# Spreading a layer's last weight conversions evenly, and moving pair preparation and reciprocal transposes by one step

## The chip, the cores and the metric

One core of a Trainium2 chip runs the whole program: clustered attention, a dense two-matrix layer, and a layer of eight experts. The metric is the device time of one execution in microseconds (us). TensorE is PE in the rows (PEld: its weight loads), VectorE DVE, ScalarE ACT, GpSimd POOL, SyncE SP; SPq is the SyncE queue, which issues most DMAs. "Granted clock" is the share of TensorE's full clock that the chip allowed: 1.00 is 2.4 GHz, 0.5 is 1.2 GHz.

## The reference, cut to what matters

```python
# attention: batch 2, 8 heads, 768 positions, head_dim 64, 16 clusters
q_assign = argmax(q_n @ c_n.T); k_assign = argmax(k_n @ c_n.T)   # normalised
scores = where(q_assign == k_assign, q @ k.T / sqrt(64), -1e9)
attn = exp(scores - max); attn = attn / (sum(attn) + 1e-9)
x = attn @ v                             # to 1536 tokens x 512
# first layer: 512 -> 2048 -> 512
h = x @ w_in; x = maximum(0.01 * h, h) @ w_out
# second layer: one of 8 experts (512 -> 1024 -> 512) per token, where x @ w_skip > 0
y = x + gate * (relu(x @ w1[e]) @ w2[e])
```

The weights of the first layer, `w_in` and `w_out`, are 64-bit floats in memory. The program takes them as pairs of 32-bit words and makes 32-bit floats of them; this is the "conversion".

## The kernel before, in words

**Attention.** Two heads form a pair, and there are eight pairs. A pair has 12 steps, r = 0 to 11, 96 in all: two halves of 384 queries, in each half three blocks of 128 queries by two heads. A step s gives each engine a fixed list, in the order of the loop `for s in range(NSTEP + 12 + LAG)`, and every engine works its list strictly in order:

- TensorE: scores of step s (`sps`, L366); six transposes of the exponentials of step s - 3 into two PSUM tiles `tps` (L423); every sixth step the transpose of the reciprocal sums, `rcps` (L401), into a tile of the same two; in even steps the value product (`avps`, L438); then one item of the preparation.
- VectorE: the row maximum `st` of the scores (L369), one or two operations of a conversion, the reciprocals, and operations of the preparation.
- ScalarE: `Abs` of a conversion in every fourth step (L557), a copy of the preparation, the two copies of `tps` to SBUF (L430), the copy of `rcps`, the exp (L384), and in steps 2 and 8 the copy `xr` of the finished value product (L446).
- GpSimd: splits into high and low parts of the next pair, the load `rb` of the reciprocals (L409) from memory, where SyncE stored them, and their product with `xr` (L453).

The preparation of a pair lies in the steps of the two pairs before it. It is a table of (step, slot, function): four raw transposes (`rawps`, L179) with a copy each in the step behind, the cluster scores (`asps`, L231), their transposes (`scps`, L243), the choice of the cluster in four VectorE operations (`argmax_0` to `argmax_3`), the transposes of the one-hot mask (`ohps`, L290), its scaling (`mk`, L296) and its DMAs. `plan(d)` writes this table with all steps relative to d. The slot "pb" stands at the end of a step on TensorE, "a0" near its start, "d" on VectorE behind the maximum.

**First layer.** 48 iterations i, 16 for each of three blocks of 512 tokens. An iteration has `up` of i (12 matmuls, L658), `down` of i - 2 (12 matmuls, L765), then `m1_act`: `lk` on ScalarE (L749), `g` on VectorE (L750), `gh` on ScalarE (L751), `gl` on VectorE (L752); then the splits of the weights of i + 2: `whii` and `whio` on ScalarE (L632, L643), `wloi` and `wloo` on GpSimd (L634, L644). `up` of i needs `whii` and `wloi` of i.

Of 32 pieces of the weights (128 rows each) 20 are converted during attention. The last 12 are converted in the first iterations by `conv_next(n)`, which brings the count of converted pieces up to n, two at a time: two `Abs` on ScalarE, then four VectorE operations for each piece (L559, L561, L564, L570). After each two it issues the next loads. The load of the fourth of the 12 goes into a tile (`stg`, two buffers) that the first of the 12 occupies. Pieces 5 to 8 of the 12 are read by `split_i` at the end of iteration 10, pieces 9 to 12 by `split_o` from there on.

Of the kernel before, what the change touches and what calls it, by code (L numbers as in the profile page):

```python
# [25 lines left out]
def kernel(  # L26
# [284 lines left out]
    def plan(d):  # L311
        return [
            (d - 8, "pb", raw_pe, 0), (d - 7, "a0", raw_act, 0), (d - 7, "pb", raw_pe, 1),
            (d - 6, "a0", raw_act, 1), (d - 6, "pb", raw_pe, 2), (d - 5, "a0", raw_act, 2), (d - 5, "pb", raw_pe, 3),
            (d - 4, "a0", raw_act, 3), (d - 4, "pb", assign_pe, None),
            (d - 3, "a0", assign_act, None), (d - 3, "pb", argmax_pe, None),
            (d - 2, "d", argmax_0, None), (d - 2, "d", argmax_1, None), (d - 1, "d", argmax_2, None),
            (d, "d", argmax_3, None), (d + 1, "pb", mask_pe, None), (d + 2, "d", mask_dve, None),
            (0, "a0", raw_split, 0), (1, "a0", raw_split, 1), (2, "a0", raw_split, 2), (3, "a0", raw_split, 3),
            (3, "d", exchange, 0), (5, "d", exchange, 1), (max(d + 2, 5), "d", mask_dma, None),  # L320
        ]

    PREP = plan(0)
    PREP0 = [(3, "a0", assign_act, None), (3, "pb", argmax_pe, None), (4, "d", argmax_0, None), (4, "d", argmax_1, None),
             (5, "d", argmax_2, None), (6, "d", argmax_3, None)]
    PREP1 = [(1, "pb", assign_pe, None), (2, "a0", assign_act, None), (2, "pb", argmax_pe, None), (3, "pb", argmax_0, None), (4, "pb", argmax_1, None), (5, "d", argmax_2, None), (6, "pb", argmax_3, None), (7, "pb", mask_pe, None), (8, "d", mask_dve, None),
             (8, "d", mask_dma, None)]
    PREPS = {0: PREP0, 1: PREP1, 2: plan(4), 3: plan(2)}

    def prep(p, r, slot):  # L330
        if p >= NP:
            return
        for rr, sl, f, arg in PREPS.get(p, PREP):
            if rr == r and sl == slot:
# [262 lines left out]
    def preps(p, r, slot):  # L597
        prep(p + 1, r, slot)
        if r >= 4:
            prep(p + 2, r - 12, slot)  # L600
# [65 lines left out]
    def load_next(n):  # L666
        while nxt[0] < min(n, len(pieces)):
            load_piece(*pieces[nxt[0]])
            nxt[0] += 1

    def conv_next(n):
        while nxt[1] < min(n, len(pieces)):
            two = pieces[nxt[1]:nxt[1] + 2]
            for i_ in range(5):
                for pc in two:
                    convert_op(*pc, i_)
            nxt[1] += 2
            load_next(nxt[1] + (2 if wsp[0] is None else 4))

    for s in range(NSTEP + 12 + LAG):  # L680
        p, r = divmod(s, 12)
        if s < NSTEP:
            st_scores(s)
        conv_step(s, 0)
        preps(p, r, "a0")
        preps(p, r, "pa")
        if 0 <= s - LAG < NSTEP:
            st_transpose(s - LAG)
            st_evac(s - LAG)
        gf, rf = divmod(s, 6)  # L690
        if 0 < gf <= NSTEP // 6:
            if rf == 2:
                recip_rows(gf - 1)
            elif rf == 3:
                nc.sync.dma_start(rscr[gf - 1], rrow_t.pop(gf - 1))
        g, kt = divmod(s - 6 - LAG, 6)
        if 0 <= g < NSTEP // 6 and kt % 2:
            st_av(g, kt - 1)
            st_av(g, kt)
        if s < NSTEP:  # L700
            st_exp(s)
        if 0 <= g < NSTEP // 6 and kt == NT - 1:
            av_evac(g)
            av_split(g)
        if 0 <= g < NSTEP // 6 and kt == 3:
            recip_load(g)
        if 0 < gf <= NSTEP // 6 and rf < 2:
            recip(gf - 1, rf)
        preps(p, r, "d")
        preps(p, r, "pb")  # L710
        if r == 10 and p + 1 < NP:
            load_v(p + 1)
        conv_step(s, 1)
        if s == NSTEP:
            att_a.release()
            rt = pool("rt", "left")
            ring_b[0] = pool("ring_b", "left")
            wip[0] = pool("wi", "left")
            for c in range(NDIR // 4, NPC // 4):
                load_f32(c)  # L720
            load_next(2)
        if s == NSTEP + 4:
            for i in range(3):
                split_i(i)
# [301 lines left out]
    for i in range(NI):  # L1026
        if i == 14:
            r_consts()
        if i >= 2:
            m1_up(i)  # L1030
        for f, arg in sorted(r_tasks.get(i, ()), key=lambda x: x[1]):
            f(arg)
        step_gen(i, 0)
        if i >= 2:
            m1_down(i - 2)
        m1_act(i)
        step_gen(i, 1)
        if i + 2 < NI:
            if i:
                split_i(i + 2)  # L1040
            split_o(i + 2)
            g_, j_ = divmod(i + 2 - 2 * NFC, 4)
            if g_ >= 0 and j_ == 3:
                load_chunk(8 + 2 * g_)
                load_chunk(9 + 2 * g_)
        conv_next(i + 3 if i % 2 else 0)

    lb = NBLK - 1
    LT = lb * TPB
# [370 lines left out]
```

## Time and profile before

| What | Value |
| --- | --- |
| median of 3 runs | 690.68 us (690.42 to 690.96) |
| the profiled execution, its own time | 689.63 us |
| its span, first to last instruction | 687.9 us |
| TensorE busy | 636.7 us, 93% of the span |
| ScalarE busy | 423.8 us, 62% |
| VectorE busy | 407.4 us, 59% |
| GpSimd busy | 278.2 us, 40% |
| mean granted clock | 0.985 |

The shares are means over stages with different limits, so they only say where to look: TensorE is the engine whose idle time can be worth something, and there are 51 us of it. What ended each of its idle stretches stands in the list of waits and in the rows in order of time, where a bracket such as "[0.39 <-ACT pt L430]" gives the idle time of the engine ahead of an instruction and what ended it.

### The profile page before, as it was taken

Reading aid. Unit: us, or ns where it says so; the run is one execution under the profiler, and the core shown is the slowest. Engines: PE = TensorE matmul, PEld = TensorE weight load, DVE = VectorE, ACT = ScalarE, POOL = GpSimd, SP = SyncE. Lnnn points to the kernel's source line nnn. Section 1 sums busy time; section 2 is a strip of 40 time slices with the busy share of each in tenths; the row PEclk is TensorE's granted clock in tenths of the full one; section 3 lists DMA queues with packets and bytes.
Section 4 is the critical chain, followed back from the end, with each engine's and each line's share of the span. In section 5 each row is a group of like instructions: output and inputs, shape, how many; then the busy total and the mean of one; then the engine's idle time right before and its main releaser. Section 6 shows DMA issues by size and latency. Waiting matters only on the chain. (4 is left out here: it accounts for less than half of the span.)

```text
span 687.9 us, 10140 instructions
## 1 busy us (share of the span) xinstructions
PE 636.7 (93%) x3587; PEld 491.8 (71%) x3587; DVE 407.4 (59%) x687; ACT 423.8 (62%) x824; POOL 278.2 (40%) x295
## 2 busy tenths in 40 slices
PE   5898999999999999499999999999999979989994
PEld 3676766666766666378888888788787868767873
DVE  5755858686776653767523213623226348999991
ACT  5887888897888885254445444445444436757870
POOL 4233636264553324363554444444444273002321
PEclk9999999999999999889999999999999999999997
DMA  8763764767656354221003000006303349989950
GB/s 196 184 189 95 196 163 140 187 172 193 167 153 171 111 183 144 104 111 61 1 3 122 1 1 0 1 0 245 122 3 122 123 163 362 339 280 333 357 192 25
DMA packets 62659, 98.31 MB, mean 143 GB/s; under 512 B 27593, under 2 KB 31659, under 8 KB 62224
## 3 DMA queue, kind: packets, MB, share of 16 engines
q1 hardware_dynamic: 59040, 88.13, 41.5%
q0 software_dynamic: 3568, 9.52, 4.2%
q8 instruction: 29, 0.48, 0.3%
q14 instruction: 22, 0.18, 0.1%
HBM read 72.47 MB, written 11.65 MB: 122 GB/s over the span
## 5 line engine op out<-in xcount | busy, mean ns | idle before, releaser
L369 DVE TENSOR_REDUCE st<-sps 128x1 f32<-128x768 f32 x96 | 91.5, 954 | 66.7 <-PE sps L366 66.3
L430 ACT ACTIVATE pt<-tps 128x384 f32<-128x384 f32 x192 | 84.8, 503 | 19.2 <-PE tps L423 18.6
L384 ACT ACTIVATE pr<-sps,st 128x768 f32<-128x768 f32 x96 | 87.7, 914 | 13.9 <-DVE st L369 13.4
L750 DVE TENSOR_TENSOR g<-ups,lk 128x512 f32<-128x512 f32 x48 | 33.1, 689 | 105.9 <-ACT lk L749 105.8
L634 POOL TENSOR_TENSOR wloi<-rawb,whii 128x512 fp32r<-128x512 f32 x36 | 46.7, 1298 | 115.4 <-ACT whii L632 115.4
L658 PE MATMUL ups<-xh,whii 128*128 128x512 f32 x192 | 76.0, 396 | 7.9 <-ACT whii L632 7.9
L423 PE MATMUL tps<-ident,pr 128*128 128x128 f32 x576 | 78.7, 273 | 0.5 <-ACT pt L430 0.5
L658 PE MATMUL ups<-xh,wloi 128*128 128x512 f32 x192 | 75.7, 394 | 1.4 <-POOL wloi L634 1.3
L658 PE MATMUL ups<-xl,whii 128*128 128x512 f32 x192 | 75.6, 394 | 0.0
L765 PE MATMUL acc<-whio,gh 128*128 128x512 f32 x184 | 73.4, 399 | 0.0
L765 PE MATMUL acc<-wloo,gh 128*128 128x512 f32 x184 | 71.8, 390 | 0.1
L423 PEld LDWEIGHTS tps<-ident,pr 128*128 128x128 f32 x576 | 68.4, 140 | 5.1 <-ACT pt L430 1.6
L438 PE MATMUL avps<-pt,vnat 128*64 128x384 f32 x384 | 71.9, 498 | 0.0
L765 PE MATMUL acc<-whio,gl 128*128 128x512 f32 x184 | 71.8, 390 | 0.0
L751 ACT ACTIVATE gh<-g 128x512 fp32r<-128x512 f32 x48 | 30.4, 632 | 51.9 <-DVE g L750 51.9
L749 ACT ACTIVATE lk<-ups 128x512 f32<-128x512 f32 x48 | 28.5, 593 | 50.9 <-PE ups L658 50.9
L752 DVE TENSOR_TENSOR gl<-g,gh 128x512 fp32r<-128x512 f32 x48 | 34.6, 721 | 33.5 <-ACT gh L751 33.5
L453 POOL TENSOR_TENSOR xr<-xr,rb 128x384 f32<-128x384 f32 x16 | 16.0, 1002 | 81.2 <-ACT xr L446 77.9
L658 PEld LDWEIGHTS ups<-xh,whii 128*128 128x128 f32 x192 | 36.6, 190 | 16.3 <-ACT whii L632 8.3
L644 POOL TENSOR_TENSOR wloo<-rawb,whio 128x512 fp32r<-128x512 f32 x36 | 47.0, 1304 | 0.8 <-ACT whio L643 0.8
L1171 POOL DMA_INDIRECT out_dram<-y,idx_s x8 | 13.6, 1695 | 76.8 <-DVE y L1169 36.0
L658 PEld LDWEIGHTS ups<-xh,wloi 128*128 128x128 f32 x192 | 36.6, 190 | 10.2 <-POOL wloi L634 2.6
(294 smaller groups left out, 1388.8 us busy)
## 6 DMA issues: line engine op xcount, KB each, us to landing
rawb<-in_moe_w_dram SPq DMA_DIRECT2D x26, 1024.0 KB, 6.9
stg<-in_moe_w_in_dram SPq DMA_DIRECT2D x16, 512.0 KB
stg<-in_moe_w_out_dram SPq DMA_DIRECT2D x16, 512.0 KB, 6.8
rawa<-in_moe_w_dram SPq DMA_DIRECT2D x8, 1024.0 KB
vnat<-in_v_dram SPq DMA_DIRECT2D x8, 384.0 KB, 3.7
rb<-recip_scratch POOLq DMA_DIRECT2D x32, 96.0 KB, 3.0
w_f_scratch<-cvt SPq DMA_DIRECT2D x12, 256.0 KB, 2.3
rawb<-w_f_scratch SPq DMA_DIRECT2D x3, 1024.0 KB
```

Of the source, the lines that this page charges most:

```text
L369: nc.vector.tensor_reduce(out=st[:, 0:1], in_=ps[:, :, 0:HS], axis=AX.XY, op=ALU.max, negate=True)
L384: nc.scalar.activation(out=pr, in_=ps[:, :, 0:HS], func=AF.Exp, bias=st[:, 0:1], accum_out=sm_t[g][:, 3 * h + j:3 * h + j + 1])
L423: nc.tensor.transpose(ps[:, t, :], pr[:, kh, t * P:(t + 1) * P], ident)
L430: nc.scalar.activation(out=pt[:, 3 * kh:3 * kh + 3, j, :], in_=t_t[s][kh], func=AF.Copy)
L438: nc.tensor.matmul(av_t[g][64 * h:64 * h + 64, :], lhsT=vnat[p][:, h, kt, :], rhs=pt_t[p, half, h][:, kt].rearrange("p j c -> p (j c)"), s ...
L634: eng.tensor_tensor(out=lo, in0=src, in1=_f(hi), op=ALU.subtract)
L644: nc.gpsimd.tensor_tensor(out=lo, in0=src, in1=_f(hi), op=ALU.subtract)
L658: nc.tensor.matmul(ps, lhsT=w[:, cc, :], rhs=x[:, cc, cs], start=(n == 0), stop=(n == 3 * KD - 1))
L750: nc.vector.tensor_tensor(out=g, in0=ps, in1=t, op=ALU.max)
L751: nc.scalar.activation(out=gh, in_=g, func=AF.Copy)
L752: nc.vector.tensor_tensor(out=gl, in0=g, in1=_f(gh), op=ALU.subtract)
L765: nc.tensor.matmul(ps, lhsT=a[:, ts_], rhs=w, start=(fc == 0 and n == 0), stop=(fc == NFC - 1 and n == 2))
```

## The change

Three edits.

- The tables of the preparation move by one step: `plan(0)` for most pairs becomes `plan(1)`, and those of pairs 2 and 3, `plan(4)` and `plan(2)`, become `plan(5)` and `plan(3)`. All items with a step relative to d move; the splits, the exchange DMAs, and mostly the mask DMAs stay.
- The transpose of the reciprocals moves from steps 2 and 8, which have a value product, to steps 3 and 9, which have none; its store moves from 3 and 9 to 4 and 10. The load of the stored rows stays.
- The 12 conversions were four at iteration 1 and two at each of 3, 5, 7 and 9. They become two at each of 1, 3, 5, 7, 8 and 9.

```diff
-    PREP = plan(0)
+    PREP = plan(1)
...
-    PREPS = {0: PREP0, 1: PREP1, 2: plan(4), 3: plan(2)}
+    PREPS = {0: PREP0, 1: PREP1, 2: plan(5), 3: plan(3)}
...
         if 0 < gf <= NSTEP // 6:
-            if rf == 2:
+            if rf == 3:
                 recip_rows(gf - 1)
-            elif rf == 3:
+            elif rf == 4:
                 nc.sync.dma_start(rscr[gf - 1], rrow_t.pop(gf - 1))
...
-        conv_next(i + 3 if i % 2 else 0)
+        conv_next({1: 2, 3: 4, 5: 6, 7: 8, 8: 10, 9: 12}.get(i, 0))
```

TensorE around step 8 of a pair in the middle, before: the transposes of step 8 first, the cluster scores `asps` at its end, then step 9.

```order
L423 MATMUL tps<-ident,pr 128x128 x6
L401 MATMUL rcps<-ident,rc_114 128x128
L438 MATMUL avps<-pt_1314,vnat 64x384
L438 MATMUL avps<-pt_1341,vnat 64x384
L438 MATMUL avps<-pt_1314,vnat 64x384
L438 MATMUL avps<-pt_1341,vnat 64x384
L231 MATMUL asps<-raw,cblk 32x384 x4
L366 MATMUL sps<-UB 128x384 x2
L366 MATMUL sps<-VB 128x384 x2
L423 MATMUL tps<-ident,pr 128x128 x6
L243 MATMUL scps<-ident,sc 128x128 x3
```

The same steps of TensorE after the change.

```order
L423 MATMUL tps<-ident,pr 128x128 x6
L438 MATMUL avps<-pt_1303,vnat 64x384
L438 MATMUL avps<-pt_1336,vnat 64x384
L438 MATMUL avps<-pt_1303,vnat 64x384
L438 MATMUL avps<-pt_1336,vnat 64x384
L179 MATMUL rawps<-ident,natk 128x128 x3
L366 MATMUL sps<-UB 128x384 x2
L366 MATMUL sps<-VB 128x384 x2
L423 MATMUL tps<-ident,pr 128x128 x6
L401 MATMUL rcps<-ident,rc_114 128x128
L231 MATMUL asps<-raw,cblk 32x384 x4
```

The reciprocal transposes `rcps` and the cluster scores `asps` now stand behind the transposes of step 9; the last raw transposes stand where `asps` was.

ScalarE in iterations 1 and 2 of the first layer, before (`cvu<-stg` is the `Abs` of a conversion).

```order
L643 ACTIVATE whio<-rawa 128x512
L557 ACTIVATE cvu<-stg 128x512 x2
L557 ACTIVATE cvu<-stg_3385 128x512
L557 ACTIVATE cvu<-stg 128x512
L749 ACTIVATE lk<-ups 128x512
L751 ACTIVATE gh<-g 128x512
L632 ACTIVATE whii<-rawb 128x512
```

ScalarE in iterations 1 to 3 after the change.

```order
L557 ACTIVATE cvu<-stg 128x512 x2
L749 ACTIVATE lk<-ups 128x512
L751 ACTIVATE gh<-g 128x512
L632 ACTIVATE whii<-rawb 128x512
L643 ACTIVATE whio<-rawb 128x512
L749 ACTIVATE lk<-ups 128x512
L751 ACTIVATE gh<-g 128x512
L632 ACTIVATE whii<-rawb 128x512
L643 ACTIVATE whio<-rawb 128x512
L557 ACTIVATE cvu<-stg_3385 128x512
L557 ACTIVATE cvu<-stg 128x512
```

The third and fourth `Abs` stood ahead of `lk` of iteration 2; now the work of iterations 2 and 3 lies between.

ScalarE in iterations 8 and 9, before.

```order
L749 ACTIVATE lk<-ups 128x512
L751 ACTIVATE gh<-g 128x512
L632 ACTIVATE whii<-rawb 128x512
L643 ACTIVATE whio<-rawb 128x512
L749 ACTIVATE lk<-ups 128x512
L751 ACTIVATE gh<-g 128x512
L632 ACTIVATE whii<-rawb 128x512
L643 ACTIVATE whio<-rawb 128x512
L557 ACTIVATE cvu<-stg_3682 128x512
L557 ACTIVATE cvu<-stg 128x512
```

ScalarE in iterations 8 and 9 after the change.

```order
L749 ACTIVATE lk<-ups 128x512
L751 ACTIVATE gh<-g 128x512
L632 ACTIVATE whii<-rawb 128x512
L643 ACTIVATE whio<-rawb 128x512
L557 ACTIVATE cvu<-stg_3664 128x512
L557 ACTIVATE cvu<-stg 128x512
L749 ACTIVATE lk<-ups 128x512
L751 ACTIVATE gh<-g 128x512
L632 ACTIVATE whii<-rawb 128x512
L643 ACTIVATE whio<-rawb 128x512
L557 ACTIVATE cvu<-stg_3764 128x512
L557 ACTIVATE cvu<-stg 128x512
```

Two `Abs`, and behind them eight VectorE operations, now stand at the end of iteration 8 as well.

## Rows read from the trace of the kernel before

**Rows 1.** Busy us and instructions of each engine by stretch; granted clock, DMA.

```profile
core 0: us, PE busy (x) PEld busy (x) DVE busy (x) ACT busy (x) POOL busy (x), PEclk, DMA share, GB/s
17.00:257.00 240.00, 225.15 (x1490) 162.79 (x1488) 164.83 (x243) 200.60 (x459) 102.57 (x132) 1.00 0.61 164
266.50:285.20 18.70, 17.24 (x74) 13.28 (x72) 12.84 (x14) 7.35 (x13) 11.33 (x11) 1.00 0.16 50
285.20:293.10 7.90, 0.02 (x1) 0.02 (x1) 4.66 (x9) 2.37 (x5) 0.00 (x0) 0.68 0.62 226
293.10:298.60 5.50, 5.37 (x13) 3.81 (x14) 3.05 (x5) 3.73 (x7) 5.10 (x4) 0.53 0.29 114
298.60:344.80 46.20, 46.20 (x205) 38.29 (x204) 30.50 (x49) 23.02 (x41) 21.01 (x17) 1.00 0.12 46
```

**Rows 2.** What TensorE waited for, whole program: us in total, times, longest.

```profile
PE rcps L401 <- ACT pt L430: 11.0, 16, 1.1
PE ups L658 <- ACT whii L632: 7.9, 1, 7.9
```

**Rows 3.** TensorE in order of time, steps 2 and 6 to 8 of a pair.

```profile
143.59 0.33 PE L401 MATMUL rcps<-ident,rc 128*128 128x128 f32 x1 [0.39 <-ACT pt L430]
...
151.63 0.59 PE L366 MATMUL sps<-UA 80*128 80x384 f32 x2
...
154.91 0.60 PE L366 MATMUL sps<-UB 80*128 80x384 f32 x2
...
156.61 0.59 PE L366 MATMUL sps<-UA 80*128 80x384 f32 x2
...
159.34 0.33 PE L401 MATMUL rcps<-ident,rc 128*128 128x128 f32 x1 [1.13 <-ACT pt L430]
```

**Rows 4.** VectorE, then ScalarE, in order of time, same pair.

```profile
139.72 0.55 DVE L268 TENSOR_TENSOR oh<-eq,mx 128x384 bf16<-128x384 f32 x1
...
144.83 0.90 ACT L384 ACTIVATE pr<-sps,st 128x768 f32<-128x768 f32 x1 [0.61 <-DVE st L369]
...
146.61 0.87 ACT L430 ACTIVATE pt<-tps 128x384 f32<-128x384 f32 x2 [0.41 <-PE tps L423]
...
157.87 0.67 ACT L557 ACTIVATE cvu<-stg 128x512 f32<-128x512 f32 x1
...
158.78 0.89 ACT L430 ACTIVATE pt<-tps 128x384 f32<-128x384 f32 x2
...
161.16 0.49 ACT L446 ACTIVATE xr<-avps 128x384 f32<-128x384 f32 x1 [0.31 <-PE avps L438]
```

**Rows 5.** GpSimd in order of time: load of the reciprocals, its first reader.

```profile
154.64 1.10 POOL L409 DMA_DIRECT2D rb<-recip_scratch  x2 [4.06 <-DMA recip_scratch<-rrow]
...
161.74 1.00 POOL L453 TENSOR_TENSOR xr<-xr,rb 128x384 f32<-128x384 f32 x1 [5.99 <-ACT xr L446]
```

**Rows 6.** SyncE queue, VectorE, ScalarE, TensorE's weight loads around the hole.

```profile
266.59 17.17 SPq L544 DMA_DIRECT2D stg<-in_moe_w_out_dram  x2
...
282.69 1.28 DVE L570 SCALAR_TENSOR_TENSOR rawb<-stg,cvt 128x512 uint32<-128x512 uint32 x2
...
287.05 0.66 ACT L557 ACTIVATE cvu<-stg 128x512 f32<-128x512 f32 x1 [6.22 <-DMA stg<-in_moe_w_out_dram]
...
294.43 0.29 PEld L658 LDWEIGHTS ups<-xh,wloi 128*128 128x128 f32 x1 [0.85 <-POOL wloi L634]
```

**Rows 7.** ScalarE, VectorE, TensorE in iterations 5 to 8 of the first layer.

```profile
307.49 1.20 ACT L557 ACTIVATE cvu<-stg 128x512 f32<-128x512 f32 x2
...
308.17 1.91 DVE L559 TENSOR_SCALAR cvu<-cvu 128x512 f32<-128x512 f32 x2 [1.11 <-ACT cvu L557]
...
313.08 0.68 DVE L750 TENSOR_TENSOR g<-ups,lk 128x512 f32<-128x512 f32 x1
...
314.33 0.62 ACT L632 ACTIVATE whii<-rawb 128x512 fp32r<-128x512 f32 x1
314.85 0.61 ACT L643 ACTIVATE whio<-rawb 128x512 fp32r<-128x512 f32 x1
...
317.63 0.39 PE L658 MATMUL ups<-xh,whii 128*128 128x512 f32 x1
```

## The prediction

> **What bounds the kernel now.** I read the stretches first: the table of busy time per engine [rows 1] says which engine ends each stage. From 17 to 257 us (attention) TensorE is busy 225 of 240 us at full clock; from 298.6 to 344.8 us (first layer, from the end of `up` of iteration 4 to the start of that of 13) it is busy all the time. Between them lies a hole: from 285.2 to 293.1 us TensorE does nothing, and then works 5.5 us at a granted clock of 0.53, the lower level. Then I read the list of waits [rows 2]: TensorE waits 11.0 us in 16 pieces for the reciprocal transposes (one per half pair), and 7.9 us once for `whii`. These two lines are what the change touches, and both lie on TensorE, so what they lose ends in the total unless a new wait takes their place. All the rest of the program follows in a fixed order, so I pass a gain on one to one.
>
> **Part A, the conversions; where the hole comes from.** At iteration 1 the old code converts four pieces at once. The rows in order of time [rows 6] show it: the SyncE queue stands 17.17 us on the load of the fourth piece, since that tile is free only when VectorE has finished the first two (last operation 282.69 + 1.28 = 283.97). The load goes out after that, and ScalarE stands 6.22 us before that piece's `Abs` at 287.05, released by the landing. Behind that `Abs` on ScalarE wait `lk`, `gh` and then `whii` of iteration 4, for which TensorE waits.
>
> What the change takes out: the third and fourth piece go to iteration 3. ScalarE then goes from the second `Abs` to `lk` at once, and VectorE takes `g` of iteration 2 at 283.97. From `g` to the end of `whii` is 1.87 us in iterations 6 to 8 (313.08 to 314.33 + 0.62, [rows 7]), so `whii` is ready at about 285.8 and TensorE is idle 0.6 us instead of 7.9: 7.3 us gained. The clock: 12 matmuls and a wait of 0.85 us for `wloi` [rows 6] took 5.5 us at the lower level; at the upper level a matmul is 46.20 / 205 = 0.225 us [rows 1], so 12 x 0.225 + 0.85 = 3.55, and 1.95 us are gained if the clock stays up. I take it that it does: from 266.5 to 285.2 us TensorE was idle 18.70 - 17.24 = 1.46 us and the clock row reads 1.00. Sum at the front: 9.25 us. The moved `Abs` comes at about 283.97 + 2.3 + 2.9 = 289.2 (the chain's lengths, below); its data landed at 287.05, in whose time nothing changes, so it is covered by 2 us.
>
> What the change puts in: two pieces at iteration 8, so that 7, 8 and 9 all convert. ScalarE and VectorE form one chain through these: from the first `Abs` to the next `g` 5.59 us (307.49 to 313.08), from `g` to the end of `whio` 314.85 + 0.61 - 313.08 = 2.38 us, less the 0.1 us by which neighbours on ScalarE overlap (314.33 + 0.62 against 314.85) [rows 7], hence 7.9 us for an iteration that converts. TensorE needs 24 x 0.225 = 5.4 us. Before, one with and one without alternate and TensorE never waits [rows 1], so both together take the chain 10.8 us at most, the one without 2.9: as long as they alternate nobody falls back. Three in a row do. The slack before is 317.63 - 314.95 = 2.7 us [rows 7]. It is smaller afterwards, since `whii` of iteration 4 came 0.6 us late and not early: TensorE is held back 0.6 + 0.85 = 1.45 us there, and after that `whii` is ready 1.2 us ahead. So at iteration 8 the chain falls 2.5 us back, 1.2 are slack, and TensorE waits 1.3 us before `up` of 11 and 0.85 inside it for GpSimd's `wloi` (the wait of [rows 6]); at iteration 9 it falls back 2.5 again against 0.85 of slack: 1.65 + 0.85. Together 4.6 us. The bounds of this term: nothing, if the slack of 2.7 us is kept and grows, and 2 x 2.5 + 2 x 0.85 = 6.7 if none is left. I take 4.6, for the rows of the chain repeat to 0.2 us. **Net of part A: 9.25 - 4.6 = 4.6 us.** That the two old places give 9.25 and only half stays is the point: six conversions of 7.9 us stand in the chain before and after, and what really goes is the wait for the DMA and the clock.
>
> **Part B, reciprocal transposes and pair preparation, one step later.** A reciprocal transpose takes the PSUM tile that the first three transposes of its own step have filled; it waits until ScalarE has copied them out. At step 2 that wait is 0.39 us, at step 8 1.13 us [rows 3]. ScalarE's rows say why [rows 4]: in step 8 an `Abs` of 0.67 us (157.87) and the copy of a raw tile stand ahead of the copies at 158.78, so PE, there at 159.34 - 1.13 = 158.21 (1.60 us into its step), has to wait. At step 2 nothing stands ahead and 0.39 us is what the copy itself takes after the transposes; that floor remains in any step.
>
> New places: step 9. Step 8 becomes a step with value product and raw transposes, 154.91 - 151.63 = 3.28 us long [rows 3], and PE arrives at 156.61 + 3.28 + 1.60 = 161.49. ScalarE: copies of step 8 done at 158.78 + 0.89 = 159.67, then an exp of 0.90, `xr` of 0.49 and a raw copy of the same size [rows 4], 161.55, then the first of two copies (half of 0.89): 162.0. Wait 0.51 us. Step 3: here VectorE matters. One more 0.55 us operation of the cluster choice (`oh`, [rows 4]) now stands ahead of the maximum of step 2, for which ScalarE's exp already waits 0.61 us (144.83); ScalarE has 0.41 us to spare before the copies of step 3 (146.61), so 0.55 - 0.41 = 0.14 us of it come through: 0.39 + 0.14 = 0.53. The first pair has one wait in the list, pairs 1 to 5 two each beside preparation, pairs 6 and 7 the other five. For the five pairs 5 x (0.53 + 0.51), for the first pair and four of the last 5 x 0.39, for the very last none (no transposes are left in its step): 5.2 + 1.95 = 7.1 us against 11.0. **Part B gains 3.9 us.** Bounds: all 16 at the floor, 6.2 us, gains 4.8; if step 9 is no better than step 8 (1.13) the five pairs lose 5 x 0.14 = 0.7 us, the others keep 11.0 - 5 x 1.52 - 1.95 = 1.45, and 0.7 us remain as a gain; below that lies only rival (5). I take 3.9, near the upper end, because the `Abs` of a conversion falls in steps 0, 4 and 8 and never in 3 or 9.
>
> At no cost: the moved transposes themselves are the same matmuls in the other sort of step. The store of the reciprocals goes out a step later on SyncE, behind one exchange, and GpSimd, which already waits 4.06 us for it before it loads the row (154.64, [rows 5]), waits longer by about that step; but its product with `xr` begins only at 161.74, 6.0 us after the load's issue ended (154.64 + 1.10), and it is `xr` from ScalarE that ends the 5.99 us of idleness there, not the load. Behind the waiting load on GpSimd stand only the splits of the next pair, needed a pair later. If that cover went, the splits of x would be late, which nobody reads before the first layer.
>
> **Sum.** 4.6 + 3.9 = 8.5 us. The profiled execution, 689.63 us (span 687.9), would go to 681.1; it lies 1.05 us under the median of the runs, so the forecast is 690.68 - 8.5 = 682.2 us.
>
> **The rivals.**
> (1) The chain has slack at 8 and 9 after all. For it: before, `whii` is 2.7 us early without any effort. Against: the chain's own length, 7.9 against 5.4. Then 9.25 + 3.9 = 13.2 us: 677.5.
> (2) Part B gives nothing: the waits stay near their mean of 0.69 us since VectorE, with three cluster operations in steps 11, 0 and 1 beside two or three conversion steps, makes every exp of steps 2 and 8 late. For it: ScalarE already waits 0.61 us there. 690.68 - 4.6 = 686.1.
> (3) VectorE's conversions at 8 and 9 are held longer by GpSimd. The first two operations of a conversion take 1.91 us in the one that I used (308.17, [rows 7]); were that doubled in each of the two, 3.8 us more: 686.0. The Trainium skill ("SBUF — State Buffer", Who interferes with whom) has a rule for this: the two engines share a port pair as an exclusive lock, and tensor_scalar can be among the operations that block. By it back-to-back conversions would meet more of GpSimd's splits, which speaks against this change.
> (4) The clock falls again at the new waits of iterations 10 to 12. The drop before came with one idle stretch of 7.9 us; the new ones are 1.3 to 1.65 us, and 1.46 us before it cost none. If it falls at both, and an iteration of 5.4 us runs at the lower level each time, that is 5.4 us more: 687.6.
> The Trainium skill ("TensorE: Matmul & The Clock Gate", HAM oscillation) warns of just this, idle gaps between bursts that bring the clock down every time; no row here shows it for gaps so short.
> (5) Slower: reciprocal transposes in the short steps. A step without value product gives ScalarE less time than it needs (an exp and two copies are 0.90 + 0.87 = 1.8 us, such a step is 156.61 - 154.91 = 1.7 with raw transposes and less without), so a late exp of step 2 or 8 is not caught up and the transpose waits for the whole backlog. Part B has to lose what A gains: 11.0 + 4.6 = 15.6 us, a mean wait of 0.98 us, is the point from which it is slower. At 1.5 us a wait, 24 us: 690.68 - 4.6 + 13 = 699.
> (6) It doesn't do what it says: the load of the fourth piece is late for iteration 3 too and the hole only moves. It has 2 us of cover; then about half of A goes, 686.
>
> **How the numbers follow.** Forecast 0.54, (1) 0.11, (2) 0.13, (3) 0.08, (4) 0.06, (5) 0.05, (6) 0.03. A measurement of this kernel can tell about 0.2%, 1.4 us, from no change. Faster: the forecast, (1), (3), (6), most of (2) and half of (4), 0.89. Within 0.2%: the rest of (2) and (4) with a small loss in part B, 0.06. Slower: (5), 0.05. The range reaches down to (1), 677.0, with both terms at their best just left out, and up past (2), to 687.8; outside are (5), half of (4) and the tails.
>
> **What would show it.** In the changed profile: the wait of 7.9 us for `whii` gone, a short one of about 0.6 in its place, and clock 1.00 throughout the first layer; new waits of 1 to 2 us for `whii` and 0.85 for `wloi` at iterations 11 and 12; the reciprocal waits at about 7 us in all, none above 0.7; attention 4 us shorter. Wrong I am if the first layer gains the full 9 us (slack in the chain), or if maxima on VectorE or exps on ScalarE show new waits in steps 2 and 8.

## The result, and the profile after

The changed kernel takes 684.67 us (median of 3 runs, 684.03 to 685.08) against 690.68 us before: a ratio of 0.9912 (95% interval 0.9889 to 0.9934), faster by 6.0 us where 8.5 were forecast. A second set of six runs gave 683.74 us against 690.05 us before on the same chip, 0.9914 (0.9897 to 0.9932). The profiled execution shown here took 685.08 us, with a span of 683.3 us.

The stretches first, as in [rows 1]: TensorE's busy time, in the first column behind the length, and the granted clock, in the third column from the right.

```profile
core 0: us, PE busy (x) PEld busy (x) DVE busy (x) ACT busy (x) POOL busy (x), PEclk, DMA share, GB/s
17.00:253.00 236.00, 224.61 (x1488) 161.34 (x1485) 163.56 (x243) 197.19 (x459) 108.43 (x132) 1.00 0.60 161
281.30:288.40 7.10, 5.89 (x25) 4.58 (x26) 4.65 (x7) 4.81 (x10) 5.27 (x4) 1.00 0.50 191
315.60:332.50 16.90, 13.05 (x54) 9.44 (x54) 13.36 (x21) 6.77 (x14) 6.45 (x6) 1.00 0.04 16
332.50:336.00 3.50, 3.50 (x10) 2.72 (x9) 0.72 (x1) 1.40 (x3) 3.09 (x3) 0.51 0.00 0
336.00:344.00 8.00, 8.00 (x36) 6.63 (x36) 2.48 (x4) 4.05 (x7) 2.54 (x2) 1.00 0.00 1
```

The attention is 3.7 us shorter: its last step starts at 250.83 us instead of 254.50. (The first stretch of each table is cut so that both hold about the same work, 1488 and 1490 matmuls.) The hole of [rows 1], 7.90 us with 0.02 busy and then 5.50 us at clock 0.53, is now one stretch of 7.10 us at clock 1.00 in which TensorE idles 1.2 us. In return, the stretch from 315.6 us idles 3.85 us where before nothing idled, and behind it 3.5 us ran at clock 0.51.

TensorE's waits over the whole program (us in total, times, longest), which answer to [rows 2]:

```profile
PE rcps L401 <- ACT pt L430: 7.0, 15, 1.0
...
PE ups L658 <- ACT whii L632: 3.2, 3, 1.3
PE ups L658 <- POOL wloi L634: 3.2, 4, 1.3
PE rawps L179 <- issue: 2.5, 2, 1.4
```

The reciprocal transposes wait 7.0 us instead of 11.0. The single wait of 7.9 us for `whii` has become three of 3.2 us in all. Of the four `wloi` waits the longest, 1.3 us, was there before as well. The two `rawps` waits, 1.1 and 1.4 us, are new in this size: of this kind the trace of before has one, of 0.9 us.

The places of [rows 3] and [rows 4], in the same pair: the reciprocal transposes of steps 3 and 9 on TensorE, then VectorE's and ScalarE's rows ahead of the first of them (in order of time on each engine).

```profile
145.77 0.33 PE L401 MATMUL rcps<-ident,rc 128*128 128x128 f32 x1 [0.72 <-ACT pt L430]
...
160.72 0.33 PE L401 MATMUL rcps<-ident,rc 128*128 128x128 f32 x1 [0.31 <-ACT pt L430]
...
141.41 0.51 DVE L268 TENSOR_TENSOR oh<-eq,mx 128x384 bf16<-128x384 f32 x1
141.85 1.16 DVE L564 SCALAR_TENSOR_TENSOR cvt<-stg,cvt 128x512 uint32<-128x512 uint32 x1
142.93 0.94 DVE L369 TENSOR_REDUCE st<-sps 128x1 f32<-128x768 f32 x1
...
143.96 0.90 ACT L384 ACTIVATE pr<-sps,st 128x768 f32<-128x768 f32 x1 [1.18 <-DVE st L369]
```

In step 9 the wait is 0.31 us where step 8 had 1.13. In step 3 it is 0.72 us, more than the 0.39 of step 2: ScalarE's exp now waits 1.18 us (before 0.61) for the maximum at 142.93, ahead of which VectorE has `oh` and a conversion's operation of 1.16 us. The copies behind that exp come late, and so does the transpose.

The place of the hole, as in [rows 6]: the SyncE queue, ScalarE, and TensorE.

```profile
262.81 17.04 SPq L544 DMA_DIRECT2D stg<-in_moe_w_out_dram  x2
...
272.60 0.57 ACT L749 ACTIVATE lk<-ups 128x512 f32<-128x512 f32 x1
280.69 0.63 ACT L751 ACTIVATE gh<-g 128x512 fp32r<-128x512 f32 x1 [7.51 <-DVE g L750]
281.22 0.61 ACT L632 ACTIVATE whii<-rawb 128x512 fp32r<-128x512 f32 x1
...
281.89 0.50 PE L658 MATMUL ups<-xh,whii 128*128 128x512 f32 x1 [0.61 <-ACT whii L632]
...
283.24 0.50 PE L658 MATMUL ups<-xh,wloi 128*128 128x512 f32 x1 [0.62 <-POOL wloi L634]
```

SyncE still stands 17.04 us at the fourth piece's load, but nobody needs that piece now. ScalarE goes from the second `Abs` to `lk` at 272.60, `g` ends its wait at 280.69, and TensorE waits 0.61 us for `whii` and 0.62 us for `wloi`.

Iterations 7 to 9, in which three converting iterations follow each other, answer to [rows 7]: `g` on VectorE at the end of each, and matmuls around the waits in `up` of iterations 11 and 12.

```profile
312.70 0.68 DVE L750 TENSOR_TENSOR g<-ups,lk 128x512 f32<-128x512 f32 x1
...
320.67 0.68 DVE L750 TENSOR_TENSOR g<-ups,lk 128x512 f32<-128x512 f32 x1
...
328.61 0.68 DVE L750 TENSOR_TENSOR g<-ups,lk 128x512 f32<-128x512 f32 x1
...
320.89 0.39 PE L765 MATMUL acc<-whio,gl 128*128 128x512 f32 x1
322.59 0.50 PE L658 MATMUL ups<-xh,whii 128*128 128x512 f32 x1 [1.31 <-ACT whii L632]
322.92 0.40 PE L658 MATMUL ups<-xl,whii 128*128 128x512 f32 x1
323.94 0.50 PE L658 MATMUL ups<-xh,wloi 128*128 128x512 f32 x1 [0.62 <-POOL wloi L634]
...
330.52 0.50 PE L658 MATMUL ups<-xh,whii 128*128 128x512 f32 x1 [1.29 <-ACT whii L632]
...
331.88 0.50 PE L658 MATMUL ups<-xh,wloi 128*128 128x512 f32 x1 [0.62 <-POOL wloi L634]
```

From one `g` to the next 7.97 and 7.94 us pass. TensorE waits 1.31 + 0.62 us, then 1.29 + 0.62 us. After the second pair of waits its clock falls. The first three matmul rows show that such a wait takes more time than its bracket says. Without a wait a matmul of this size starts about 0.23 us after the one ahead of it, though its row is 0.39 us long. Here the start at 322.59 lies 1.70 us behind the one at 320.89, 1.47 more than that, and the next follows after 0.33.

### The profile page after: what moved, and what is told of

Read it like the earlier page. It is cut to its first block, busy times and chain, and to the rows that moved or that the text cites. A ratio compares the mean times of both kernels' runs of the same rounds, so it can differ in the third digit from the quotient of the medians.

```text
span 683.3 us, 10129 instructions
## 1 busy us (share of the span) xinstructions
PE 639.8 (94%) x3587; PEld 492.6 (72%) x3587; DVE 407.6 (60%) x687; ACT 419.7 (61%) x824; POOL 283.9 (42%) x295
## 5 line engine op out<-in xcount | busy, mean ns | idle before, releaser
L658 PEld LDWEIGHTS ups<-xh,wloi 128*128 128x128 f32 x192 | 36.4, 189 | 12.7 <-POOL wloi L634 5.0
L978 DVE TENSOR_TENSOR xl<-rawb,xh 128x1024 fp32r<-128x1024 f32 x36 | 42.3, 1217 | 0.3 <-ACT xh L976 0.3
```

The costliest lines, as they stand in the source:

```text
L658: nc.tensor.matmul(ps, lhsT=w[:, cc, :], rhs=x[:, cc, cs], start=(n == 0), stop=(n == 3 * KD - 1))
L978: eng.tensor_tensor(out=lo, in0=src, in1=_f(hi), op=ALU.subtract)
```

## The experiments

All times are medians; the kernel before, run beside each on the same chip, took 689.8 to 690.1 us.

### Each half alone

Only the new places of the conversions, in the kernel before:

```diff
-        conv_next(i + 3 if i % 2 else 0)
+        conv_next({1: 2, 3: 4, 5: 6, 7: 8, 8: 10, 9: 12}.get(i, 0))
```

> The kernel before with the new places of the twelve conversions alone (nothing in attention changes). Theory: in the changed kernel the start of up of iteration 5 gained 9.2 us over attention and the start of up of 13 only 2.5, so this kernel is 2.5 us faster than before: 688.2 us, with new waits of 1.3 us for whii and 0.6 for wloi before and in up of 11 and 12, and the granted clock at its lower level for about 3.4 us there. Rival: the drop of the clock was an accident of one run; then it is 4.4 us faster, 686.3, with clock 1.00 throughout the first layer.

Measured: 687.0 us (9 runs, 685.11 to 689.4), ratio 0.9968 (0.9956 to 0.9981), 2.9 us faster. The profiled execution is the fastest of the nine. In it the clock stays up through the first layer, the waits are the same as in the changed kernel (1.28 + 0.63 and 1.30 + 0.62), and `up` of iteration 13 starts at 340.40 instead of 344.83: 4.4 us, close to the 4.6 of part A's sum (0.3 of them lie ahead of `up` of 0, where nothing was changed). So the profile shows what the rival said, a gain of 4.4 us at full clock. The median lies 1.9 us above that execution, between the two expectations, and the runs spread over 4.3 us.

Only the attention's edits, that is the changed kernel with the old places of the conversions:

```diff
-        conv_next({1: 2, 3: 4, 5: 6, 7: 8, 8: 10, 9: 12}.get(i, 0))
+        conv_next(i + 3 if i % 2 else 0)
```

> The kernel before with the moved preparation and the moved reciprocal transposes alone (conversions as before). Theory: 3.7 us faster than before, 687.0 us; 15 waits of the reciprocal transposes of 7.0 us in all, and two waits of raw transposes of 2.5 us. Rival: the two parts are not independent, and the gain of 6.0 us came from one of them; then this one is under 1 us or over 5 us faster.

Measured: 686.82 us (6 runs), ratio 0.9953 (0.9938 to 0.9967), 3.0 us faster. The hole is there as before (7.55 us for `whii`). The last attention step starts at 251.46 instead of 254.50. The halves add up: 2.9 + 3.0 = 5.9, and both together gave 6.0.

### Three converting iterations in a row

The changed kernel with a pause between all of them:

```diff
-        conv_next({1: 2, 3: 4, 5: 6, 7: 8, 8: 10, 9: 12}.get(i, 0))
+        conv_next({1: 2, 3: 4, 5: 6, 7: 8, 9: 10, 11: 12}.get(i, 0))
```

> The changed kernel with the last four conversions at iterations 9 and 11 instead of 8 and 9, so that iterations with and without a conversion alternate throughout. Theory: the chain of ScalarE and VectorE never falls behind TensorE, and the 6.7 us lost at iterations 10 to 12 (3.8 of waits, 2 of clock, the rest restarts) come back: 684.7 - 6.7 = 678.0 us, no wait for whii after iteration 4 and clock 1.00. Rival: the loss is that of six conversions however they are placed, or the last two come too late for the splits of iterations 12 and 13: then 681 or more, with the waits at iterations 12 to 14.

Measured: 677.14 us (5 runs, 676.53 to 679.35), ratio 0.9824 (0.9807 to 0.9840), 12.7 us faster than before. TensorE from ahead of `up` of 4 to behind `up` of 13 (columns as in [rows 1]):

```profile
281.00:343.00 62.00, 60.88 (x267) 49.60 (x268) 41.23 (x63) 30.88 (x57) 32.88 (x31) 1.00 0.20 73
```

The theory held: the clock stays at 1.00, and the 1.12 us of idle time are the waits at `up` of 4. The starts of `up` of iterations 10 to 13 lie 5.47, 5.44 and 5.47 us apart. In the changed kernel they lie 6.94, 7.93 and 8.08 us apart, in the kernel before 5.44. So what the late part loses comes from the row of three, and all of it can be avoided.

### What part B is made of

Only the reciprocal transposes and their store, in the kernel before:

```diff
-            if rf == 2:
+            if rf == 3:
                 recip_rows(gf - 1)
-            elif rf == 3:
+            elif rf == 4:
```

> The kernel before with the reciprocal transposes (and their store) moved from steps 2 and 8 to 3 and 9, the preparation left where it was. Theory: the wait at step 3 of 0.72 us in the changed kernel comes from the preparation's operation on VectorE ahead of the maximum of step 2; without that move all waits lie at the floor of 0.25 to 0.4 us, and the two waits of raw transposes stay at the 0.9 us of before: 16 x 0.35 = 5.6 us against 11.0, 5.4 us faster than before: 685.3. Rival: the preparation had to leave step 8 for the transposes to profit (cluster scores and their copy stand in steps 8 and 9); then the waits at step 9 stay near 1 us and it gains 2 us or less, 688.7.

Measured: 684.0 us (5 runs), ratio 0.9918 (0.9905 to 0.9932), 5.9 us faster, as much as the whole change brings. TensorE's waits:

```profile
PE rcps L401 <- ACT pt L430: 5.7, 15, 1.2
...
PE rawps L179 <- issue: 2.0, 2, 1.0
```

The VectorE rows and the ScalarE row that answer to those of step 2 above:

```profile
138.33 0.55 DVE L268 TENSOR_TENSOR oh<-eq,mx 128x384 bf16<-128x384 f32 x1
...
142.50 0.95 DVE L369 TENSOR_REDUCE st<-sps 128x1 f32<-128x768 f32 x1
...
143.55 0.90 ACT L384 ACTIVATE pr<-sps,st 128x768 f32<-128x768 f32 x1 [0.98 <-DVE st L369]
```

`oh` stands a step earlier here, at 138.33, and the exp of step 2 waits 0.98 us instead of 1.18. The reciprocal transposes wait 5.7 us in all: 0.38 to 0.44 in step 3 of four of the pairs, 1.25 in that of one, and 0.25 in most of the others.

Only the preparation, in the kernel before:

```diff
-    PREP = plan(0)
+    PREP = plan(1)
...
-    PREPS = {0: PREP0, 1: PREP1, 2: plan(4), 3: plan(2)}
+    PREPS = {0: PREP0, 1: PREP1, 2: plan(5), 3: plan(3)}
```

> The kernel before with the preparation tables moved by one step alone; reciprocal transposes and conversions as before. Theory: the move of the preparation costs time by itself, as the difference of the runs with both attention edits (686.8) and with the reciprocal transposes alone (684.0) says: 2 to 2.8 us slower than before, 692 to 692.7, with two new waits of raw transposes of 1.1 to 1.4 us behind the mask scaling on VectorE in pairs 1 and 2, and a longer wait at step 2. Rival: the preparation only costs where the reciprocal transposes stand in steps 3 and 9; alone it is within 0.5 us of before, since the cluster scores leave step 8.

Measured: 690.2 us (12 runs), ratio 1.0005 (0.9996 to 1.0014). My theory, a loss of 2 to 2.8 us, missed, and the rival held; the preparation by itself costs and brings nothing. TensorE's waits:

```profile
PE rcps L401 <- ACT pt L430: 10.7, 16, 1.1
...
PE rawps L179 <- issue: 3.0, 2, 1.6
```

The reciprocal waits stay (10.7 us) and two raw transposes wait 3.0 us. Beside the moved reciprocals it does cost: in the six profiles with both edits the last attention step starts at 250.3 to 251.6, mean 250.8, in the two with the reciprocals alone at 249.5 and 248.6 (in the first of these the clock was low from 21 to 25 us). That is 1.8 us. The waits account for 1.8: 7.0 - 5.7 at the reciprocals, 2.5 - 2.0 at the raw transposes. The run times of the two versions on one chip lie 2.8 us apart (686.82 and 684.0); where the rest goes isn't shown.

The raw transposes wait for a PSUM tile. In the changed kernel, TensorE, then VectorE:

```profile
89.33 0.52 PE L179 MATMUL rawps<-ident,natq 128*128 128x128 f32 x3 [1.36 <-issue]
...
88.23 0.42 DVE L561 TENSOR_SCALAR cvt<-cvu 128x512 uint32<-128x512 uint32 x1
88.56 0.67 DVE L296 TENSOR_SCALAR mk<-ohps,msc 128x384 fp32r<-128x384 bf16 x1
```

The program gives `rawps` and the mask's transposes `ohps` the same tile, which is free when the scaling `mk` has read it (88.56 + 0.67 = 89.23); the raw transposes start 0.1 us later. `mk` stands behind a conversion's operation in VectorE's row. The profile names no cause for the wait ("issue"); I read it from these times. The changed kernel with the preparations of pairs 2 and 3 where they were:

```diff
-    PREPS = {0: PREP0, 1: PREP1, 2: plan(5), 3: plan(3)}
+    PREPS = {0: PREP0, 1: PREP1, 2: plan(4), 3: plan(2)}
```

> The changed kernel, with preparation steps 4 and 2 put back on the step numbers that they had before; the other preparation steps and the reciprocal transposes stay moved. Theory (the two raw transposes that wait 1.12 and 1.36 us at 61.5 and 89.3 wait for a mask scaling that the moved steps put late in VectorE's row): both waits fall under 0.5 us, and the attention ends about 1.5 us earlier, at 249.3 instead of 250.8; 683.2 us. Rival (those waits come from the masks' own place, not from where steps 2 and 4 stand): waits and time stay as in the changed kernel, 684.7 us, step 95 at 250.8.

Measured: 683.64 us (5 runs), ratio 0.9905 (0.9890 to 0.9919). The waits came out at 1.03 (at 33.9 us) and 0.93 (at 60.9), not under 0.5; together 0.5 us less, and the last attention step starts 1.0 us earlier. With the old step numbers such waits exist as well, again 0.1 us longer than an `mk` (which ends at 33.83 and 60.81), so the theory had the tile right and the size wrong. The run time can't be told from the changed kernel's 683.74 and 684.67.

The last of the four operations of the cluster choice one step earlier, so that it no longer stands ahead of the maximum of step 2:

```diff
-            (d, "d", argmax_3, None), (d + 1, "pb", mask_pe, None), ...
+            (d - 1, "d", argmax_3, None), (d + 1, "pb", mask_pe, None), ...
```

> The changed kernel with the last operation of the cluster choice on VectorE (oh) one step earlier, in step 0 behind the one before it, instead of in step 1. Theory: this operation, ahead of the maximum of step 2, makes the 0.72 us wait of the reciprocal transposes at step 3; without it the wait falls to 0.25 to 0.45 us in pairs 2 to 6, some 1.5 to 2 us in all: 683 us. Rival: VectorE is as late with the maximum of step 2 through the conversions and the other operations; waits at step 3 stay at 0.6 us or more and the time at 684.5.

Measured: 693.74 us (6 runs), ratio 1.0059 (1.0040 to 1.0079): 9 to 10 us slower than the changed kernel, and both expectations missed. VectorE, ScalarE and TensorE of a pair, in order of time on each:

```profile
142.93 1.37 DVE L268 TENSOR_TENSOR oh<-eq,mx 128x384 bf16<-128x384 f32 x1
...
144.87 0.94 DVE L369 TENSOR_REDUCE st<-sps 128x1 f32<-128x768 f32 x1
...
145.90 0.90 ACT L384 ACTIVATE pr<-sps,st 128x768 f32<-128x768 f32 x1 [1.14 <-DVE st L369]
...
148.85 0.90 ACT L384 ACTIVATE pr<-sps,st 128x768 f32<-128x768 f32 x1 [1.19 <-DVE st L369]
...
150.66 0.33 PE L401 MATMUL rcps<-ident,rc 128*128 128x128 f32 x1 [1.99 <-ACT pt L430]
```

And two stretches of the attention (columns as in [rows 1]):

```profile
117.00:124.00 7.00, 6.67 (x34) 4.28 (x35) 2.97 (x5) 4.66 (x12) 4.14 (x5) 0.76 0.53 146
182.00:190.00 8.00, 7.61 (x40) 5.27 (x41) 3.89 (x6) 5.61 (x14) 4.16 (x5) 0.79 0.68 183
```

`oh` now runs beside a subtraction on GpSimd (`VA`, 142.87 to 143.88) and takes 1.37 us instead of 0.51. The maximum of step 1 comes late, and two exps in a row wait (1.14 and 1.19 us) where one did. ScalarE gets no step to catch up in, and the reciprocal transpose of step 3 waits 1.99 us. There are four waits of this length. After two of them, at 117.3 and 182.4 us, the granted clock fell in the middle of the attention; after those at 150.7 and 215.8 it stayed at 1.00. VectorE's rows in steps 0 to 2 show no idle time, and the place of a single 0.5 us operation among them is worth microseconds. So this run doesn't test what it was meant to: whether `oh` alone makes the wait of 0.72 us at step 3 in the changed kernel stays open.

### The hole: DMA or chain

The kernel before, with the fourth piece loaded into the other set of tiles, so that its load waits for nothing:

```diff
-        if wsp[0] is None or a % 2:
+        if wsp[0] is None or a < 2:
             t = ring_a.tile([P, 512, 2], U32, tag="stg", name="stg", bufs=2)
```

> The kernel before with the third and fourth of the last twelve pieces loaded into the two buffers of the other stage tile, so that the fourth load does not wait for the first conversions; all conversions stay where they were. Theory: the hole of 7.9 us at iteration 4 is mostly the two extra conversions in the chain, and 3 us of it the wait for the landing; VectorE then runs through all four (to about 289) and whii comes at about 290.8: a hole of 5 to 6 us, the clock still falls, 2 to 3 us faster than before: 687.4. Rival: the wait for the DMA is the hole; then it shrinks below 3 us, the clock stays up and the time is about 682.

Measured: 688.22 us (8 runs), ratio 0.9975 (0.9964 to 0.9987), 1.7 us faster. ScalarE, then TensorE:

```profile
280.51 0.67 ACT L557 ACTIVATE cvu<-stg 128x512 f32<-128x512 f32 x1 [0.75 <-DVE cvt L561]
...
289.47 0.63 ACT L751 ACTIVATE gh<-g 128x512 fp32r<-128x512 f32 x1 [7.81 <-DVE g L750]
...
277.40 0.79 PE L765 MATMUL acc<-wloo,gh 128*128 128x512 f32 x1 [2.36 <-POOL wloo L644]
...
290.67 0.67 PE L658 MATMUL ups<-xh,whii 128*128 128x512 f32 x1 [3.54 <-ACT whii L632]
```

The expectation from the chain held but for the gain (1.7 us instead of 2 to 3); the other, 682 us, missed. The `Abs` no longer waits for a landing, yet `gh` still waits 7.81 us for `g`, and TensorE 2.36 and 3.54 us. VectorE works through all four conversions first. From `up` of 0 to `up` of 5 this version takes 31.84 us where before took 34.82, with the clock down at two places of it; the changed kernel takes 25.63. So the DMA wait is about 3 of the 9.2 us at the front. Of the other 6.2 some 1.1 us are still the clock: from `up` of 4 to `up` of 5 it is 7.52 us here and 6.46 in the changed kernel. The largest part, about 5 us, is that two conversions leave the chain there, and they come back at iterations 8 and 9.

### The clock

Six matmuls of 128x128 that nobody reads, ahead of `up` of 11 and 12 in the changed kernel, where TensorE waits:

```diff
+        if i in (11, 12):
+            wb_ = bank("misc", 1, "wps0", [P, P])
+            for _ in range(6):
+                nc.tensor.matmul(wb_, lhsT=ident, rhs=ident, start=True, stop=True)
         if i >= 2:
             m1_up(i)
```

> The changed kernel, with six extra matmuls of 128x128 in fp32 ahead of up(11) and up(12), on data that is there, into a PSUM tile that nothing reads; the output is the same. They fill the two waits of 1.3 us for whii. Theory (TensorE's drop of 332.6 to 336.0 in the changed kernel follows from these waits): no lower clock in the first layer, and the runs come about 2 us lower, near 682.7 us, with less spread. Rival (the drop is not brought about by these waits): a drop in the first layer again in the profile, and 684.7 us or up to 1 us more for what the extra matmuls take.

Measured: 682.13 us (4 runs, 681.23 to 683.17), ratio 0.9887 (0.9872 to 0.9903). No lower clock in the first layer; `up` of 13 starts 74.1 us behind `up` of 0, against 75.9 in the changed kernel.

The unaltered changed kernel and this version again, on one chip:

> The changed kernel once more, unaltered, for the spread of its times and a second profile, beside the filled version on the same chip. Theory (the two waits of 1.3 us for whii let TensorE's clock fall in some executions, not in all): the times spread over 2 us or more around 684.5 us; this profile has the lower clock in the first layer or not, and without it the start of up(13) lies 74.1 us behind that of up(0), with it 75.9. Rival (the drop follows from the waits every time): again a stretch of 3.4 us at the lower clock at about 332 us, and 75.9.

> The version with six extra matmuls ahead of up(11) and up(12) once more, on the same chip as the unaltered changed kernel. Theory (filling the two waits keeps the clock up): no lower clock in the first layer, up(13) 74.1 us behind up(0), and the median 1 to 2 us under that of the unaltered one. Rival (its 682.1 us was chance): medians within 0.5 us of each other.

Measured: 683.74 us (6 runs, 683.32 to 685.36) unaltered, 683.22 us (6 runs, 681.21 to 684.45) filled. A stretch of 3.5 us in the first layer of the unaltered one (columns as in [rows 1]):

```profile
324.70:328.20 3.50, 3.38 (x8) 2.71 (x9) 3.48 (x6) 0.81 (x2) 1.48 (x2) 0.51 0.00 0
```

And the whole row of converting iterations in the filled one:

```profile
315.10:336.50 21.40, 20.15 (x98) 16.21 (x98) 15.28 (x24) 9.88 (x19) 9.54 (x8) 1.00 0.03 11
```

The clock fell in the unaltered one again, but one iteration earlier, and `up` of 13 starts 74.4 us behind `up` of 0. There the lower clock cost 0.2 us: TensorE would have waited for the chain of ScalarE and VectorE anyway, and the wait for `whii` of iteration 12 is gone instead. In the first profile it fell behind the last wait, where nothing hides it, and cost 1.75. In the filled version it stays up, in both profiles. It stayed up too in the profiles of two versions with the same unfilled waits (the conversions alone, and the one with the old preparations), and fell in that with the earlier `argmax_3`. So after such a pair of waits (1.3 and 0.6 us) the clock falls in some executions and not in others. A single wait of 1.3 us stands ahead of `up` of 3 in 13 of the 14 profiles, and after that one it never fell. Two filled profiles without a fall, against two of five unfilled, are too few to show that the filling keeps the clock up. That it brings 1 to 2 us didn't come out: the medians on one chip differ by 0.5 us, less than either set spreads.

### The two good parts together

The kernel before with the reciprocals' move and the alternating places; the preparation stays where it was:

```diff
-            if rf == 2:
+            if rf == 3:
                 recip_rows(gf - 1)
-            elif rf == 3:
+            elif rf == 4:
...
-        conv_next(i + 3 if i % 2 else 0)
+        conv_next({1: 2, 3: 4, 5: 6, 7: 8, 9: 10, 11: 12}.get(i, 0))
```

> The kernel before with the two edits that the runs so far showed to pay: reciprocal transposes at steps 3 and 9, the preparation left alone, and conversions at iterations 1, 3, 5, 7, 9 and 11. Theory: the two add up, 5.9 us of the one and 9.7 us of the other (677.1 against 686.8 with both attention edits): 689.9 - 15.6 = 674.3 us. Rival: they meet (less attention time leaves the loads of the last pieces less time); then 676 or more with a wait of ScalarE for a landing piece in iterations 1 to 11.

Measured: 676.38 us (5 runs, 675.50 to 677.29), ratio 0.9803 (0.9789 to 0.9817): 13.6 us under the kernel before, and 7.4 to 8.3 under the changed one. TensorE from `up` of 5 to `up` of 13 (columns as in [rows 1]):

```profile
286.10:329.80 43.70, 43.70 (x193) 35.84 (x193) 31.39 (x49) 21.70 (x40) 21.26 (x16) 1.00 0.20 73
```

Its waits over the whole program:

```profile
PE rcps L401 <- ACT pt L430: 5.7, 15, 1.2
...
PE ups L658 <- POOL wloi L634: 1.9, 2, 1.3
```

TensorE is busy 43.70 of 43.70 us at full clock. The time came 2 us above what the sum of the parts gave, where the rival had it, but without the rival's sign: ScalarE waits for no piece to land. At `up` of 13 the profiled execution is 15.0 us ahead of before, near the sum's 15.6; it loses 0.9 us behind that.

## Why the prediction was right, and where its size was off

The time lies in the range, 2.5 us above the forecast. The mechanism held for the conversions and for the reciprocals; it was wrong for the preparation, and errors that cancel helped. Each half by the runs: part A was to bring 4.6 us and brought 2.9, part B 3.9 and brought 3.0.

**Part A, the front.** Forecast 9.25 us from `up` of 0 to `up` of 5. In the profile of before that takes 301.31 - 266.49 = 34.82 us, after 288.35 - 262.72 = 25.63: 9.19 us. The idle rest (0.61 and 0.62 us, forecast 0.6 and 0.85) and the clock (1.00) came as worked out. Wrong is only what I said of its nature, that the wait for the DMA and the clock are what really goes: with that wait alone taken out, 3.0 us of the 9.2 came, and 1.7 us in the run time. With the clock's share the two make about 4, and two conversions that leave the chain make the rest.

**Part A, the late loss.** Forecast 4.6 us. From `up` of 5 to `up` of 13 it is 43.52 us before, 50.25 after: 6.7. The chain's 7.9 us held (7.97, 7.94). The waits are in the places forecast and a little shorter: 1.31 + 0.62 + 1.29 + 0.62 = 3.84, against 1.3 + 0.85 + 1.65 + 0.85. In executions without a fall of the clock the loss is nevertheless 5.1 us (the version with the conversions alone: 48.60 - 43.52), 0.5 over the forecast, since each wait takes about 0.3 us more than its bracket (1.47 and 0.10 against 1.31 in the rows above). The rest, 1.6 us, is the clock behind the last wait.

**Rival (4)** thus came true, each time in one of its two places. I had it at 5.4 us and a chance of 0.06, and that price is half of what its words say: an iteration of 5.4 us at half the clock loses 5.4 us each time, 10.8 for two. It costs 0.2 or 1.75 us, depending on where in the row of waits it falls, and it came in both profiles of the changed kernel. My reason against it was 1.46 us of idleness before without a fall, most of it one wait of 1.29 us at 279.89. That wait brought no fall in any later profile either, but it isn't like the new ones, which come in pairs of 1.3 and 0.6 us. The Trainium skill ("TensorE: Matmul & The Clock Gate", HAM oscillation) warns of idle gaps that bring the clock down between bursts of matmuls. Its example has waits of 3 to 5 us, longer than those that I applied it to; here pairs of 1.3 and 0.6 us were followed by a fall in three of five profiles.

**Rival (1)** had the right price for another schedule: the slack that I denied the row of three is there when converting iterations alternate, and that version came to 677.14 us against its 677.5.

**Part B.** Forecast 7.1 us of waits for the reciprocals, measured 7.0. That is luck: it hides two errors that cancel. Step 9 is better than forecast (0.31 instead of 0.51 us), and the 0.39 us that I took for a floor in any step is none: waits of 0.25 are common. So the reciprocals alone could bring 5.9 us, more than the 4.8 that I gave as the most. Step 3 is worse (0.72 instead of 0.53): I let 0.14 us of `oh` through to the transpose, but with `oh` a step earlier it waits 0.43, so the moved preparation, with `oh` ahead of the maximum, costs 0.29. An exp of step 2 that waits longer for its maximum is what I had named as the sign against me; of its growth from 0.61 to 1.18 us, 0.37 came with the reciprocals' move alone (0.98). The attention got 3.7 us shorter in the first profile and 2.9 in the second, which is 0.8 us late from the first pairs on.

The step that failed is that I costed the preparation's move at nothing, or thought it part of the gain. It brings nothing alone. Beside the other it costs about 1.8 us of attention, 2.8 in run time: longer waits at step 3, where `oh` in the way of the maximum is the likely cause but wasn't isolated, and raw transposes that wait for `mk` to free their PSUM tile. Of VectorE's moved operations I had counted only `oh`.

**What stays open.** Behind the first layer the profiles differ, though nothing there was changed. A stretch of 75 us around the routing of tokens, in the kernel before (columns as in [rows 1]):

```profile
545.00:620.00 75.00, 67.42 (x371) 53.50 (x369) 59.68 (x133) 45.84 (x62) 22.50 (x16) 0.98 0.77 270
```

The same in the changed kernel:

```profile
545.00:620.00 75.00, 67.97 (x358) 54.28 (x358) 61.88 (x142) 43.79 (x60) 20.12 (x16) 0.91 0.81 288
```

From `up` of 47 to the end it is 145.5 us before and 147.1 after (146.9 in the second profile). It goes with the clock: over all 14 profiles it is 144.9 to 145.5 us in the four with a mean of 0.98 in this stretch, and 146.7 to 147.1 in the five with 0.91. One of these five is the version before with only the fourth piece's load moved, and the alternating version, with all the changed attention, has 0.93 and 145.6 us. So the attention's edits don't bring it about by themselves; whether the times of arrival do, or chance, wasn't settled. In the first profile, 4.0 us over the 681.1 us that I forecast for it, this is 1.6 us and the late loss 2.1.

## What to carry to other kernels

Work that stands in a chain between two engines should alternate with steps that leave it out, and an even count per step doesn't do that: the same twelve pieces cost 6.6 to 7.5 us more with three full steps in a row than with a pause between them. Where an edit has several parts, price each alone with all three engines' rows, since a part that looks neutral may take back what another gives: here the reciprocals' move alone brings 5.9 us, and with the preparation moved as well 3.0. A wait on the bottleneck can cost more than its length, where the clock falls behind it; that fall costs least where the engine would have waited again anyway.

## What the runs showed of the hardware that I had not expected

- TensorE's granted clock fell to its lower level after pairs of waits of 1.3 and 0.6 us between matmuls at full load, in three of five profiles with such waits unfilled (0.51 over 3.5 us), and after two of four waits of 1.99 us in the attention (0.76 and 0.79 as the mean of 7 and 8 us). It did not fall after single waits of 1.3 us ahead of `up` of 3 (13 profiles), nor after 1.12, 1.36 and 1.64 us in the attention.
- One VectorE operation on 128x384 (`oh`) took 0.51 us in one place and 1.37 us in another, there beside a GpSimd subtraction. The two `L561` operations of a conversion took 2.92 us in iteration 1 of the first layer, beside GpSimd's `wloi` and `wloo` (274.48 to 277.36), and 0.75 us in iterations 7 to 9, where GpSimd's last operation had ended 0.2 us earlier. All this is in the changed kernel, but for the 1.37 us, which stand in the version with the earlier `argmax_3`. That GpSimd is the cause is likely and was not tested.
